# Strided attention feeding an FFN on one core: a new loop order for the strided copies to x^T, and one mask for a whole strided pair

## The chip, the cores and the metric

The kernel runs on one core of a Trainium2 chip. A core has TensorE (PE, matmuls), VectorE (DVE), ScalarE (ACT), GpSimd (POOL) and a queue engine (SP) that issues transfers; each engine works through its own list of instructions in order, and they wait for each other by semaphores. The metric is the device time of one execution, in microseconds (us).

## The reference

Eight batches of eight heads, 576 tokens, 64 values per head. Heads 0 to 3 see the last 32 tokens ("local"), heads 4 to 7 see the earlier tokens of the same class modulo 32 ("strided", at most 18 tokens a class). Then a gated FFN with no bias.

```python
scores = q @ k^T / sqrt(64)
rel = pos[:, None] - pos[None, :]
mask_local   = (rel >= 0) & (rel < 32)                  # heads 0..3
mask_strided = (rel >= 0) & (pos[None, :] % 32 == pos[:, None] % 32)   # heads 4..7
attn = softmax(where(mask, scores, -1e9));  o = attn @ v
x = o as [4608, 512]
out = (((x @ w1) * (x @ w2)) @ w3) @ w_out
```

## The kernel before, in words

w3 and w_out are folded into one matrix `w34` near the start, so each of the nine tiles of 512 tokens needs two products with w1 and w2 (L496, L507), their product on VectorE (L510) and one product with `w34` (L523). The FFN reads x^T, held as four tiles `xT`, one for each pair of heads.

Attention goes by pairs of heads: in each batch two local pairs (p0, p1) and two strided ones (p2, p3). Batches 0 and 1 use an older path (`ah_...`), at the start. From batch 2 on (`s.b >= AHEAD`) a strided pair puts its tokens in five chunks: four of 126 tokens (XW), of which chunk c (0 to 3) holds the tokens t*32 + a*4 + c with t = 0..17 and a = 0..6; and one chunk of 72 (SQ) with the tokens of a = 7. In each chunk a token sees only those of its own class.

The steps of a pair, each a function:

- `ph_S` (L308): the scores, transposed, into two PSUM tiles, `sps` for all chunks but the last, `pt` for the last chunk. The same `pt` also takes the transposes of the next pair's q and k (`ph_T`), which are then copied to `qT` and `kT` (L77 and L79 are the line of a helper `copy`, for ScalarE and VectorE). Where the next pair is the first of a batch, `ph_T` also brings the last 64 tokens of all its heads ("rest").
- `ph_soft`: exp on ScalarE (L328), in two instructions, for the first chunks and the last, to `pte`; then the masks on VectorE (L331) to `ptm`. A local pair needs one multiplication of 128x1152; a strided one has two, 126x1008 with `maskX` (126 columns, repeated eight times) and 72x144 with `maskS` (72 columns, twice).
- `ph_PV` (L344): `ptm` times v, with a column of ones beside v that gives the sums; `norm` divides on VectorE (L453 reciprocal, L454 to `xqs`).
- `ph_T2` (L462): transposes back, into one PSUM tile `ps`, and the copy to `xT`. For a local pair VectorE copies 576 contiguous values (L79). For a strided pair ScalarE copies twice: 504 values of the chunks of 126 (L470), and 72 values of the last chunk (L471). Within a row of `xT` token t*32 + a*4 + c is a value of two bytes at that place, while `ps` holds (c, t, a) in order.

PE's order is written out by hand. A list `stream` holds, for each pair, scores with the next pair's transposes, six gaps, PV, five gaps, T2, one gap. `host` spreads the FFN's parts of the tile before into these gaps. So an FFN tile and the attention of the batch that the next tile needs run interleaved, and in a batch PE comes to PV of p3 twelve L523 matmuls after its scores, and to T2 of p3 ten matmuls after PV. On the other engines a scheduler settles the order when the kernel is compiled.

The masks are made once. `maskS` comes at the start (L109). `maskX` is made just ahead of batch 2's own first pair, as the product of a small PE matmul (`xps`) with a causal triangle, on VectorE (L751).

Of the kernel before, what the change touches and what calls it, by code (L numbers as in the profile page):

```python
# [9 lines left out]
FP16 = mybir.dt.float16  # L10
AF = mybir.ActivationFunctionType
# [3 lines left out]
def _ap(t: bass.AP, off_add, dims):  # L15
    return bass.AP(tensor=t.tensor, offset=t.offset + off_add, ap=dims)
# [3 lines left out]
def kernel(  # L20
# [11 lines left out]
    nc = tc.nc  # L32
    B, H, S, D = q.shape
# [3 lines left out]
    P = 128  # L37
# [4 lines left out]
    scale = 1.0 / float(D) ** 0.5  # L42
# [5 lines left out]
    LQ, LT = 96, 6  # L48
    SQ, ST = 72, 8
# [4 lines left out]
    LC = 384  # L54
    XW, XN = 126, 4
    XC = XW * XN
# [3 lines left out]
    consts = ctx.enter_context(tc.tile_pool(name="consts", bufs=1))  # L60
# [11 lines left out]
    def pe(ins):  # L72
        return tc.keep_in_program_order(ins)

    def copy(eng, out, in_):
        if eng == "a":
            nc.scalar.copy(out=out, in_=in_)  # L77
        elif eng == "v":
            nc.vector.tensor_copy(out=out, in_=in_)  # L79
        else:  # L80
            nc.gpsimd.tensor_copy(out=out, in_=in_)  # L81
# [6 lines left out]
    maskL = consts.tile([P, LQ], FP16)  # L88
# [16 lines left out]
    maskS = consts.tile([SQ, SQ], FP16)  # L105
# [12 lines left out]
    v16S = [t[0:SQ].rearrange("p (h c e) -> p h c e", h=4, c=ST) for t in v16R]  # L118
    v16X = [t[:, 0:16 * (D + 1)].rearrange("p (h c e) -> p h c e", h=4, c=XN) for t in v16R]
    v16Y = [t[0:SQ, 16 * (D + 1):20 * (D + 1)].rearrange("p (h e) -> p h e", h=4) for t in v16R]  # L120
    maskX = consts.tile([XW, XW], FP16)


    qT = consts.tile([P, 4, S], FP16)
# [108 lines left out]
    for b in range(B):  # L233
        for hp in range(4):
            s = Pair()
# [62 lines left out]
    def ph_S(s):  # L298
        w, kr, n, n1 = s.w, s.kr, s.n, s.n1
        sps = psB.tile([P, 2, NB], FP32, tag="big", name="sps")  # L300
        pt = psB.tile([P, 2, NB], FP32, tag="big", name="pt")
        s.ps = sps

        def sc(h, c):
            r = half_rows(h)
            l = w if c < n1 else s.wl
            o = sps[:, h, c * w:c * w + l] if c < n1 else pt[:, h, LC:LC + l]
            pe(nc.tensor.matmul(o, kT[r, s.hp, w * c:w * c + P], qT[r, s.hp, w * c:w * c + l],  # L308
                                start=True, stop=True))

        for i in range(n):
            sc(0, (i - 1) % n)
            sc(1, i)

        def soft():
            ph_soft(s, pt)

        return pt, soft

    def ph_soft(s, pt):  # L320
        w, kr, n, n1 = s.w, s.kr, s.n, s.n1
        sps = s.ps
        pte = att.tile([P, 2 * S], FP16, tag="pte", bufs=2)
        ptm = s.ptm = ptms[s.hp % 2]
        m1 = 2 * n1 * w
        kl = kr if s.local else SQ
        for r, lo, hi, src in ((kr, 0, m1, sps[0:kr, 0:2, 0:n1 * w]), (kl, m1, 2 * S, pt[0:kl, :, LC:LC + s.wl])):
            nc.scalar.activation(out=pte[0:r, lo:hi], in_=src, func=AF.Exp, bias=0.0, scale=scale)  # L328
        for r, lo, hi, x, mk in (((P, 0, 2 * S, LQ, maskL),) if s.local else
                                 ((XW, 0, m1, XW, maskX), (SQ, m1, 2 * S, SQ, maskS))):  # L330
            nc.vector.tensor_mul(ptm[0:r, lo:hi].rearrange("p (a x) -> p a x", x=x),  # L331
                                 pte[0:r, lo:hi].rearrange("p (a x) -> p a x", x=x),
                                 _ap(mk, 0, [[mk.ap[0][0], r], [0, (hi - lo) // x], [1, x]]))

    def ph_PV(s):
        w, kr, n, n1 = s.w, s.kr, s.n, s.n1
        vt = (v16L if s.local else v16X)[s.b % 2]
        s.xqs = att.tile([P, ST, 2, D], FP16, tag="xqs", bufs=2, name="xqs")
        for c in range(n):
            for h in range(2):  # L340
                hv = 2 * (s.hp % 2) + h
                c0 = (h * n1 + c) * w if c < n1 else 2 * n1 * w + h * s.wl
                k, vv = (SQ, v16Y[s.b % 2][:, hv]) if not s.local and c == XN else (kr, vt[0:kr, hv, c, :])
                pe(nc.tensor.matmul(s.ps[:, h, c * 65:c * 65 + 65], s.ptm[0:k, c0:c0 + P], vv,  # L344
                                    start=True, stop=True))
        norm(s, s.ps[0:w, :, 0:n * 65], 0, n)
# [102 lines left out]
    def norm(s, xv, c0, l):  # L449
        w = s.w  # L450
        rcp = att.tile([P, 2, ST], FP32, tag="rcp")
        xv = xv.rearrange("p h (i e) -> p h i e", e=65)
        nc.vector.reciprocal(out=rcp[0:w, :, 0:l], in_=xv[:, :, :, D])  # L453
        nc.vector.tensor_mul(s.xqs[0:w, c0:c0 + l].rearrange("p i h d -> p h i d"), xv[:, :, :, 0:D],  # L454
                             _ap(rcp, 0, [[rcp.ap[0][0], w], [ST, 2], [1, l], [0, D]]))

    def ph_T2(s):
        w, n = s.w, s.n
        ps = psM.tile([P, 1024], FP16, tag="m")
        for t in range(n):  # L460
            l = w if t < n - 1 else s.wl
            pe(nc.tensor.transpose(ps[:, t * w:t * w + l],  # L462
                                   s.xqs[0:l, t].rearrange("p h d -> p (h d)"),
                                   id16[0:l, 0:l]))
        o = xT[s.hp][:, S * s.b:S * s.b + S]
        if s.local:
            copy("a" if s.b < AHEAD else "v", o, ps[:, 0:S])
        elif w == XW:
            ov = o.rearrange("x (t a c) -> x c t a", a=8, c=4)
            nc.scalar.copy(out=ov[:, :, :, 0:7], in_=ps[:, 0:XC].rearrange("x (c t a) -> x c t a", c=4, a=7))  # L470
            nc.scalar.copy(out=o.rearrange("x (t r) -> x t r", r=32)[:, :, 28:32],  # L471
                           in_=ps[:, XC:S].rearrange("x (t c) -> x t c", c=4))
        else:
            nc.scalar.copy(out=o.rearrange("x (p c) -> x p c", c=n),  # L474
                           in_=ps[:, 0:S].rearrange("x (c p) -> x p c", p=w))
# [4 lines left out]
    def ab_parts(tch):  # L480
        tok = bass.ds(tch * NT, NT)
        res = []

        def first():
            abts[tch] = ffn.tile([P, KF, NT], FP16, tag="abt", bufs=4, name=f"abt{tch}")

        for jc in range(KF):
            st = {}

            def a(qt, jc=jc, st=st):  # L490
                if qt == 0:
                    if jc == 0:
                        first()
                    st["a"] = psF.tile([P, NT], FP32, tag="f", name="aps")
                for ci in (2 * qt, 2 * qt + 1):
                    pe(nc.tensor.matmul(st["a"], w1h[:, ci, bass.ds(jc * P, P)], xT[ci][:, tok],  # L496
                                        start=(ci == 0), stop=(ci == KM - 1)))
                if qt:
                    asb = ffn.tile([P, NT], FP32, tag="asb")
                    nc.scalar.copy(out=asb, in_=st["a"])  # L500
                    st["asb"] = asb

            def bb(qt, jc=jc, st=st):
                if qt == 0:
                    st["b"] = psF.tile([P, NT], FP32, tag="f", name="bps")
                for ci in (2 * qt, 2 * qt + 1):
                    pe(nc.tensor.matmul(st["b"], w2h[:, ci, bass.ds(jc * P, P)], xT[ci][:, tok],  # L507
                                        start=(ci == 0), stop=(ci == KM - 1)))
                if qt:
                    nc.vector.tensor_mul(abts[tch][:, jc, :], st["b"], st["asb"])  # L510

            res += [lambda f=f, qt=qt: f(qt) for f in (a, bb) for qt in range(2)]
        return res
# [15 lines left out]
    def o_parts(tch):  # L529
        res = []  # L530
        for ts in range(NT // P):
            def done(ps, ts=ts):
                osb = ffn.tile([P, DM], FP32, tag="osb", bufs=3)
                nc.scalar.copy(out=osb, in_=ps)  # L534
                nc.scalar.dma_start(out_r[tch * (NT // P) + ts], osb)

            if tch + 1 < NTILE or ts + 1 < NT // P:
                res += acc_parts(lambda ci, ts=ts: abts[tch][:, ci, bass.ds(ts * P, P)],
                                 lambda ci: w34[:, ci, :], done, 4)
        return res  # L540
# [80 lines left out]
    add(ah_PV, p1, 0)  # L621
    add(ah_PV, p1, 1)
    add(ph_T2, p0)
    add(ah_T, p2)
    add(ph_T2, p1)
# [23 lines left out]
    for p, s in enumerate(pairs):  # L649
# [3 lines left out]
        t = pairs[p + 1] if p + 1 < len(pairs) else None  # L653
# [86 lines left out]
    causalX = selX[0:XW, P:P + XW]  # L740
# [7 lines left out]
                            pattern=[[1, XW]], channel_multiplier=-1)  # L748
    xps = psF.tile([P, 512], FP32, tag="f", name="mxps")
    pe(nc.tensor.matmul(xps[0:XW, 0:XW], selX[0:7, 0:XW], selX[0:7, 0:XW], start=True, stop=True))  # L750
    nc.vector.tensor_mul(maskX, xps[0:XW, 0:XW], causalX)  # L751
    tile1 = ab_parts(1) + o_parts(1)
    stream[pos[0]]()
    tile1[0]()
# [54 lines left out]
```

## Time and profile before

Three runs took 282.64, 283.52 and 285.09 us; the median is 283.52. The profiled execution took 282.21 us, of which the span from the first to the last instruction is 280.5.

| | us | note |
|---|---|---|
| profiled execution | 282.21 | span 280.5, TensorE clock granted in full |
| PE busy | 261.0 | 93% of the span |
| VectorE busy | 148.7 | 53% |
| ScalarE busy | 157.0 | 56% |
| GpSimd busy | 114.0 | 41%, none after 185 us |
| L470, copies of 504 to x^T | 17.4 | 12 of 1450 ns, all on ScalarE |
| L471, copies of 72 to x^T | 4.3 | 12 of 357 ns |
| L331, strided masks | 9.7 and 6.0 | 12 of 809 ns, 12 of 500 ns on average |
| L331, local masks | 11.0 | 12 of 915 ns on average |
| L328, exp | 12.2 and 3.4 | strided pairs: 12 of 1015 ns, 12 of 281 ns |

How to read it: a group's mean covers instructions that ran alone and ones that ran beside others. The shortest of the masks are 682 and 219 ns (strided) and 759 ns (local), the longest 1392, 1066 and 1421 ns. The profile names an instruction by its line, engine, operation and tiles; what an engine waited for is inferred from semaphores. Idle time of an engine that is not the bottleneck costs nothing by itself.

### The profile page before, as it was taken

Reading aid. Unit: us, or ns where it says so; the run is one execution under the profiler, and the core shown is the slowest. Engines: PE = TensorE matmul, PEld = TensorE weight load, DVE = VectorE, ACT = ScalarE, POOL = GpSimd, SP = SyncE. Lnnn points to the kernel's source line nnn. Section 1 sums busy time; section 2 is a strip of 40 time slices with the busy share of each in tenths; the row PEclk is TensorE's granted clock in tenths of the full one; section 3 lists DMA queues with packets and bytes.
Section 4 is the critical chain, followed back from the end, with each engine's and each line's share of the span. In section 5 each row is a group of like instructions: output and inputs, shape, how many; then the busy total and the mean of one; then the engine's idle time right before and its main releaser. Section 6 shows DMA issues by size and latency. Waiting matters only on the chain.

```text
span 280.5 us, 6375 instructions
## 1 busy us (share of the span) xinstructions
PE 261.0 (93%) x2477; PEld 135.2 (48%) x2477; DVE 148.7 (53%) x306; ACT 157.0 (56%) x322; POOL 114.0 (41%) x139
## 2 busy tenths in 40 slices
PE   1789999999899999998998999999999999999995
PEld 0465455555455445544554455445544544444442
DVE  2665342747677448745875477467447743320320
ACT  2663335766655765576656665766676664333322
POOL 4677775878817837648349258100000000000000
PEclk9999999999999999999999999999999999999999
DMA  7999999998749599299399396210031003004003
GB/s 208 271 336 390 394 385 241 246 218 211 267 161 252 147 313 280 71 275 307 54 271 278 131 271 193 112 41 2 1 115 40 0 25 127 0 0 153 0 0 150
DMA packets 60170, 48.65 MB, mean 173 GB/s; under 512 B 31324, under 2 KB 50988, under 8 KB 60140
## 3 DMA queue, kind: packets, MB, share of 16 engines
q1 hardware_dynamic: 54956, 38.87, 53.0%
q10 hardware_dynamic: 5184, 9.37, 8.9%
q8 instruction: 19, 0.31, 0.5%
q14 instruction: 11, 0.09, 0.1%
HBM read 38.80 MB, written 9.44 MB: 172 GB/s over the span
## 4 chain that ended last, share of the span: by engine, by line
PE 55%; DMA 13%; ACT 10%; DVE 9%; issue 8%; POOL 2%; SPq 1%; ACTq 1%; POOLq 0%; DVEq 0%
PE bps L507 18%; PE aps L496 17%; PE ops L523 10%; DMA st<-in_moe_w_out_dram 4%; DMA st<-in_k_dram 4%; ACT pte L328 3%; DMA st<-in_moe_w_dram 3%; DVE ptm L331 3%; PE ps L462 3%; PE sps L344 3%; DVE xqs L454 2%; DVE kT L79 2%; DMA st<-in_v_dram 2%; ACT osb L534 2%; ACT xT L471 2%
## 5 line engine op out<-in xcount | busy, mean ns | idle before, releaser
L507 PE MATMUL bps<-xT,w2h 128*128 128x512 f16 x288 | 76.2, 379 | 0.0
L496 PE MATMUL aps<-xT,w1h 128*128 128x512 f16 x288 | 75.1, 380 | 1.2 <-ACT xT L474 0.7
L510 DVE TENSOR_TENSOR abt<-bps,asb 128x512 f16<-128x512 f32 x72 | 49.4, 686 | 37.7 <-PE bps L507 28.0
L523 PE MATMUL ops<-w,abt 128*128 128x512 f16 x280 | 67.1, 379 | 0.0
L500 ACT COPY asb<-aps 128x512 f32<-128x512 f32 x72 | 42.3, 599 | 42.9 <-PE aps L496 33.6
L81 POOL CAST t<-st 128x1024 f16<-128x1024 f32 (+1 forms) x46 | 46.1, 1009 | 32.2 <-DMA st<-in_q_dram 17.0
L496 PEld LDWEIGHTS <-w1h 128*128 128x128 f16 x288 | 26.5, 98 | 29.7
L507 PEld LDWEIGHTS <-w2h 128*128 128x128 f16 x288 | 26.2, 98 | 28.3 <-issue 1.2
L523 PEld LDWEIGHTS <-abt 128*128 128x128 f16 x280 | 25.3, 98 | 26.3
L199 POOL CAST v16L<-st 32x768 f16<-32x768 f32 (+1 forms) x32 | 27.5, 860 | 8.4 <-DMA st<-in_v_dram 6.0
L328 ACT ACTIVATE pte<-sps 128x960 f16<-128x960 f32 (+1 forms) x24 | 23.9, 994 | 11.9 <-PE sps L308 11.9
L470 ACT COPY xT<-ps 128x504 f16<-128x504 f16 x12 | 17.4, 1450 | 18.8 <-PE ps L462 18.8
L534 ACT COPY osb<-ops 128x512 f32<-128x512 f32 x35 | 20.8, 594 | 12.7 <-PE ops L523 12.3
L331 DVE TENSOR_TENSOR ptm<-pte,maskL 128x1152 f16<-128x1152 f16 x12 | 11.0, 915 | 24.6 <-ACT pte L328 24.6
L331 DVE TENSOR_TENSOR ptm<-pte,maskX 126x1008 f16<-126x1008 f16 x12 | 9.7, 809 | 23.8 <-ACT pte L328 23.8
L454 DVE TENSOR_TENSOR xqs<-sps,rcp 96x768 f16<-96x768 f32 (+1 forms) x24 | 21.3, 889 | 0.8
L77 ACT COPY qT<-pt 128x224 f16<-128x224 f16 (+4 forms) x60 | 17.6, 352 | 4.8 <-DVE kT L79 4.4
L79 DVE COPY kT<-pt 128x512 f16<-128x512 f16 (+4 forms) x48 | 14.1, 325 | 4.5 <-ACT qT L77 3.1
L462 PEld LDWEIGHTS <-xqs 96*128 96x128 f16 (+2 forms) x188 | 11.3, 97 | 10.1 <-DVE xqs L454 4.0
L523 PE MATMUL ops<-woh,w3T 128*128 128x512 f16 x64 | 15.7, 380 | 0.2 <-DVE w3T L567 0.2
L344 PEld LDWEIGHTS <-ptm 128*128 128x128 f16 (+2 forms) x264 | 10.6, 97 | 10.8 <-DVE ptm L331 8.0
L462 PE MATMUL ps<-id,xqs 96*128 96x96 f16 (+2 forms) x188 | 13.5, 207 | 1.7 <-DVE xqs L454 1.6
(104 smaller groups left out, 262.8 us busy)
## 6 DMA issues: line engine op xcount, KB each, us to landing
out_dram<-osb ACTq DMA_DIRECT2D x35, 256.0 KB
st<-in_q_dram SPq DMA_DIRECT2D x16, 512.0 KB
st<-in_k_dram SPq DMA_DIRECT2D x16, 512.0 KB
st<-in_moe_w_dram SPq DMA_DIRECT2D x16, 512.0 KB
st<-in_v_dram SPq DMA_DIRECT2D x32, 144.0 KB
st<-in_v_dram SPq DMA_DIRECT2D x24, 112.0 KB
st<-in_moe_w_out_dram SPq DMA_DIRECT2D x4, 512.0 KB
st<-in_q_dram SPq DMA_DIRECT2D x8, 128.0 KB
```

Of the source, the lines that this page charges most:

```text
L81: nc.gpsimd.tensor_copy(out=out, in_=in_)
L199: nc.gpsimd.tensor_copy(out=vt[pr, hs, :, 0:D], in_=st[pr])
L328: nc.scalar.activation(out=pte[0:r, lo:hi], in_=src, func=AF.Exp, bias=0.0, scale=scale)
L331: nc.vector.tensor_mul(ptm[0:r, lo:hi].rearrange("p (a x) -> p a x", x=x), pte[0:r, lo:hi].rearrange("p (a x) -> p a x", x=x), _ap(mk, 0, ...
L454: nc.vector.tensor_mul(s.xqs[0:w, c0:c0 + l].rearrange("p i h d -> p h i d"), xv[:, :, :, 0:D], _ap(rcp, 0, [[rcp.ap[0][0], w], [ST, 2], [ ...
L462: pe(nc.tensor.transpose(ps[:, t * w:t * w + l], s.xqs[0:l, t].rearrange("p h d -> p (h d)"), id16[0:l, 0:l]))
L496: pe(nc.tensor.matmul(st["a"], w1h[:, ci, bass.ds(jc * P, P)], xT[ci][:, tok], start=(ci == 0), stop=(ci == KM - 1)))
L500: nc.scalar.copy(out=asb, in_=st["a"])
L507: pe(nc.tensor.matmul(st["b"], w2h[:, ci, bass.ds(jc * P, P)], xT[ci][:, tok], start=(ci == 0), stop=(ci == KM - 1)))
L510: nc.vector.tensor_mul(abts[tch][:, jc, :], st["b"], st["asb"])
L523: pe(nc.tensor.matmul(st["ps"], lhs(ci), rhs(ci), start=(ci == 0), stop=(ci == KF - 1)))
L534: nc.scalar.copy(out=osb, in_=ps)
```

## The change

Five places are edited, all of them for strided pairs from batch 2 on, but that the layout of `pte` and `ptm` is also changed for local ones.

- `ph_T2`: both copies to x^T run through (c, a, t), with the token class's 18 values of t innermost, where before the first ran through (c, t, a) and the second through (t, c). In `xT` the step of the innermost loop is now 32 values (64 bytes); before it was 4 values (8 bytes) in the first copy, and in the second the four values of c were adjacent. The number of values is as it was.
- `maskX` has 576 columns: four copies of the 126 columns, and `maskS` in the last 72, with zeros below it (partitions 72 to 125).
- `ph_soft`: `pte` and `ptm` hold head 0 in columns 0 to 575 and head 1 in 576 to 1151, all five chunks in a row, and one multiplication of 126x1152 takes the place of the two. The exp of the last chunk works on 126 partitions, before on 72.
- `ph_PV`: the column of a chunk follows the new layout; the matmuls are the same.
- Where `maskX` is made: a memset, four multiplications in place of one, and a copy of `maskS`.

```diff
-    maskX = consts.tile([XW, XW], FP16)
+    maskX = consts.tile([XW, S], FP16)
...
-        m1 = 2 * n1 * w
-        kl = kr if s.local else SQ
-        for r, lo, hi, src in ((kr, 0, m1, sps[0:kr, 0:2, 0:n1 * w]), (kl, m1, 2 * S, pt[0:kl, :, LC:LC + s.wl])):
-            nc.scalar.activation(out=pte[0:r, lo:hi], in_=src, func=AF.Exp, bias=0.0, scale=scale)
-        for r, lo, hi, x, mk in (((P, 0, 2 * S, LQ, maskL),) if s.local else
-                                 ((XW, 0, m1, XW, maskX), (SQ, m1, 2 * S, SQ, maskS))):
-            nc.vector.tensor_mul(ptm[0:r, lo:hi].rearrange("p (a x) -> p a x", x=x),
-                                 pte[0:r, lo:hi].rearrange("p (a x) -> p a x", x=x),
-                                 _ap(mk, 0, [[mk.ap[0][0], r], [0, (hi - lo) // x], [1, x]]))
+        pv = pte.rearrange("p (h x) -> p h x", h=2)
+        for lo, hi, src in ((0, n1 * w, sps[0:kr, 0:2, 0:n1 * w]), (n1 * w, S, pt[0:kr, :, LC:LC + s.wl])):
+            nc.scalar.activation(out=pv[0:kr, :, lo:hi], in_=src, func=AF.Exp, bias=0.0, scale=scale)
+        x, mk = (LQ, maskL) if s.local else (S, maskX)
+        nc.vector.tensor_mul(ptm[0:kr, 0:2 * S].rearrange("p (a x) -> p a x", x=x),
+                             pte[0:kr].rearrange("p (a x) -> p a x", x=x),
+                             _ap(mk, 0, [[mk.ap[0][0], kr], [0, 2 * S // x], [1, x]]))
...
-                c0 = (h * n1 + c) * w if c < n1 else 2 * n1 * w + h * s.wl
+                c0 = h * S + c * w
...
-            ov = o.rearrange("x (t a c) -> x c t a", a=8, c=4)
-            nc.scalar.copy(out=ov[:, :, :, 0:7], in_=ps[:, 0:XC].rearrange("x (c t a) -> x c t a", c=4, a=7))
-            nc.scalar.copy(out=o.rearrange("x (t r) -> x t r", r=32)[:, :, 28:32],
-                           in_=ps[:, XC:S].rearrange("x (t c) -> x t c", c=4))
+            ov = o.rearrange("x (t a c) -> x c a t", a=8, c=4)
+            nc.scalar.copy(out=ov[:, :, 0:7], in_=ps[:, 0:XC].rearrange("x (c t a) -> x c a t", c=4, a=7))
+            nc.scalar.copy(out=ov[:, :, 7], in_=ps[:, XC:S].rearrange("x (t c) -> x c t", c=4))
...
-    nc.vector.tensor_mul(maskX, xps[0:XW, 0:XW], causalX)
+    nc.vector.memset(maskX[:, XC:S], 0.0)
+    for c in range(XN):
+        nc.vector.tensor_mul(maskX[:, c * XW:(c + 1) * XW], xps[0:XW, 0:XW], causalX)
+    nc.vector.tensor_copy(out=maskX[0:SQ, XC:S], in_=maskS)
```

## The prediction

> **What bounds the kernel now.** I read the page's engine table first, then the waits of PE, then the timeline around the strided pairs. PE is busy for 261.0 of 280.5 us, at full granted clock, so only the time in which PE stands still can be won.
>
> ```profile
> PE 261.0 (93%) x2477; PEld 135.2 (48%) x2477; DVE 148.7 (53%) x306; ACT 157.0 (56%) x322; POOL 114.0 (41%) x139
> ```
>
> By the windows view 11.7 us of PE's idle time lie before 76 us, where input transfers and start-up chains rule, and 3.3 us behind 277, the last output; this change touches neither much. From 76 to 237 us the timeline (start, length, engine, line, operation; in brackets the idle time before it and what ended that) shows PE's idle stretches, which I add up by cause. All but one are of three kinds:
>
> ```profile
> 96.36 0.27 PE L344 MATMUL sps<-v16S,ptm 126*128 126x65 f16 x3 [0.60 <-DVE ptm L331]
> ...
> 99.11 0.43 PE L462 MATMUL ps<-id,xqs 126*128 126x126 f16 x5 [0.33 <-DVE xqs L454]
> ...
> 130.94 0.54 PE L344 MATMUL sps<-v16L,ptm 128*128 128x65 f16 x12 [0.86 <-DVE ptm L331]
> ```
>
> First kind: PV of the second strided pair (p3) waits for its mask: 0.60, 0.39 and 0.15 = 1.14 us in all. Second: T2 of p3 waits for the normalised rows `xqs`: 0.33, 0.24, 0.33, 0.22, 0.24 = 1.36 us. Third: PV of the next batch's first local pair waits for its mask, 0.20, 0.86, 0.18, 0.18, 0.18 = 1.60 us. Once, at the end, the FFN waits 0.50 us for the last copy to x^T (L471). Together 4.6 us: that is all that this stage can give. The first and third kinds hang on ScalarE: `pte` (exp) stands in its queue behind the two copies to x^T of the pair before:
>
> ```profile
> 119.41 1.45 ACT L470 COPY xT<-ps 128x504 f16<-128x504 f16 x1 [1.56 <-PE ps L462]
> 120.56 0.36 ACT L471 COPY xT<-ps 128x72 f16<-128x72 f16 x1
> 120.74 0.60 ACT L534 COPY osb<-ops 128x512 f32<-128x512 f32 x1
> 121.23 1.02 ACT L328 ACTIVATE pte<-sps 126x1008 f16<-126x1008 f32 x1
> ```
>
> The scores for that exp were ready at about 120.2; it starts at 121.23. So ScalarE's two copies are on the path, and what they cost decides.
>
> **Part 1: the copies to x^T.** ScalarE copies that write contiguously lie on a line: 56 elements 218 ns, 512 elements 595, 576 elements (L474) 642, so 172 ns + 0.827 ns per element. Some of them read PSUM with 128-byte (L77) or 144-byte (L474) steps and still lie on it, so the new stepped read of PSUM is costed at nothing. L470 writes single fp16 values 8 bytes apart; by the line its 504 elements are 588 ns, it takes 1450: 862 ns too many, or 2.54 ns per element. L471, with groups of four adjacent values 64 bytes apart, ends 57 ns after L470 (120.92 against 120.86): its 72 elements go at 0.8 ns each, 3.2 ns for each group. From the start of L470 to the next instruction 1.33 us pass.
>
> After the change all 576 values are written singly, 64 bytes apart. No ScalarE row shows that, so bounds:
>
> - Low end: the line for both. The nearest row for single fp16 writes at a wide step is VectorE's memset of every 65th value (130 bytes), L130 and L132 below (shortest, median and longest ns): 24 values 78 ns, 32 values 85 ns, so under 1 ns for each further one. Then the two copies take 576 x 0.827 + 2 x 0.10 (between two `asb` copies in a row, 1.12 us for both, 0.525 us pass from start to start, 0.10 more than 512 x 0.827) = 0.68 us: x = -0.65 us per strided pair.
>
> ```profile
> L470 ACT COPY xT<-ps x12: 1436/1449/1460, 91.7 to 234.7; 128x504 f16<-128x504 f16 x12
> ...
> L130 DVE MEMSET v16L<- x2: 78/78/78, 1.1 to 1.3; 128x24 f16 x2
> ...
> L132 DVE MEMSET v16S<- x2: 85/85/85, 1.2 to 2.0; 126x32 f16 x2
> ```
>
> - Middle: 2.54 ns for each single value wherever it goes. L470 stays, L471 pays 72 x (2.54 - 0.8): x = +0.12.
> - High end: each new place costs what a group of L471 costs, 3.2 ns. 504 x (3.2 - 2.54) + 72 x (3.2 - 0.8) = 0.33 + 0.17: x = +0.50.
>
> I take the low end: of the two rows with wide steps both go fast (0.8 and under 1 ns per value), and only the row with the 8-byte step is slow, which looks like a cost of neighbouring writes that don't join.
>
> The Trainium skill (SBUF — State Buffer, Specifications) speaks against this change: lines of 16 bytes, two hits in a line needed for full speed, and each change of line paid. By it the old step of 8 bytes would be free and the new one not; the trace disagrees on the first half (1450 ns, not 588). Charging L470's 862 ns to its 288 line changes (3.0 ns each), the new copies would pay 504 and 72 of them: x = +0.86, and the sum below would be about +8.7 us.
>
> **Part 2: the mask.** Before: 684 + 224 ns, from 122.29 to 123.11 where GpSimd is idle. After: one operation of 126x1152, for which the local mask (128x1152, 765 ns) is the row: it ends 0.055 us before the second and 0.085 after the first, on which PV's first eight matmuls wait. So about +0.06 us where PV comes directly behind it (four of six batches, if the copies stay as slow as they are). Where GpSimd works beside it the old pair takes 0.92 + 0.85 (149.78 to 151.47), and the local mask 1.42 at worst; the merged one should end some 0.3 us earlier, twice. The exp of 126 instead of 72 partitions costs the same (281 ns). The new rows of `pte` cost nothing.
>
> **Part 3: the order on VectorE.** In the compiled instruction lists the four `kT` rest copies (0.54 us, behind a wait of 0.63 for `qT`) stand ahead of reciprocal and `xqs` of p3 before, and behind them after, in the five batches that have a next one:
>
> ```profile
> 124.34 0.54 DVE L79 COPY kT<-pt 128x128 f16<-128x128 f16 x4 [0.63 <-ACT qT L77]
> 124.80 0.21 DVE L453 RECIPROCAL rcp<-sps 126x10 f32<-126x10 f32 x1
> 125.04 0.82 DVE L454 TENSOR_TENSOR xqs<-sps,rcp 126x640 f16<-126x640 f32 x1
> ```
>
> `xqs` then starts at about 123.95 instead of 125.04 and ends at 124.8; PE reaches T2 at 125.68, when its ten matmuls are done. The second kind of stall goes: -1.36 us. What is moved back, `kT`, ends near 125.3; the scores that need it come at 126.7 (now with a wait of their own): 1.4 us of cover. On ScalarE an output's issue (0.34 us on the queue) moves ahead of the `qT` rest copies; the same cover hides it.
>
> **Part 4: making the mask.** Three more multiplications of 289 ns (L751's row) stand in VectorE's queue behind the `xqs` that ends at 71.92; they end by 72.8, the next mask comes at 73.63, and the PE matmul that now waits for their PSUM buffer comes at 73.70. Hidden by that idle time (1.71 us); without it, 0.9 us. The memset and the copy of `maskS`, some 0.1 us each (memset row 85 ns, `biasS` row 170 ns), fall to idle VectorE at 2.3 us and ahead of `kT` at 8.27; the next `kT` copy has 0.26 us of idle time before it. Nothing to +0.1.
>
> **Sum.** With x = -0.65 exp starts that much earlier, so the third kind (1.60) goes but for perhaps 0.1 beside GpSimd, the first (1.14) too, but for 0.2, and the last 0.50: 1.5 + 0.94 + 0.5 + 1.36 = 4.3, less 0.1 to 0.2 in the start: -4.1 us. What is late next is nothing before PE itself. Even half of that x gives about -3.4, since most stalls are short: the gain is capped. The profiled run took 282.21 us (span 280.5), 1.3 us below the median 283.52 of the three shown (282.64 to 285.09): 282.21 - 4.1 = 278.1, and **279.4 us** on the scale of the median.
>
> **The rivals.**
>
> - *A single write costs the same at any step* (x = +0.12). For: 2.54 ns is a plain price per value. Against: the memset row. Stalls of the second kind go (-1.36), the first gains 0.6 from the merged mask twice and loses 0.06 four times, and 0.12 is paid at 12 places (six PVs of p3, five of the next local pair, the end): -1.36 - 0.36 + 1.44 + 0.1 = -0.2: 283.3 us.
> - *Each new place is charged* (x = +0.50). For: the step is eight times wider, so nothing can join, and the bound from L471 allows it. Against: groups at the same 64-byte step ran without a surcharge. The exp has no slack (it already waits behind the copies), so 12 x 0.50 - 1.36 - 0.36 + 0.1 = +4.4: 287.9 us, slower. It turns slower than before from x = +0.14 on, by over 1% from x = +0.37. The Trainium skill's line rule (SBUF — State Buffer, Specifications) stands beside this rival, with the +8.7 given above: about 292.
> - *The copies get faster, but the time goes elsewhere*: the stalls are short (0.18 to 0.86 us) and PE's queue may hide or show them otherwise; with half the gain, 281.4 us.
>
> **Chances.** Forecast 0.50; same price 0.16; half the gain 0.10; each place charged 0.24, a third of it above the price from L471. The range runs from 277.6 (all 4.6 us gone from the profiled run's own 282.21) to 288.0 (the place-charged rival at its price), which leaves out what is charged above that price, and a little below. A change of 1%, about 2.8 us, is what a measurement of this kernel can tell from none. Faster by over 1%: the forecast and a bit of the half gain, 0.52; within 1%: 0.25; slower: 0.23.
>
> **What would show it.** The two copies' rows on ScalarE: 590 and 230 ns if right, 1450 and 350 or more if the price is per value, 1770 and 400 or more if each place is charged. T2's wait for `xqs` gone in every batch whatever the copies do. The merged mask at 765 ns, once per strided pair. PV's waits for `ptm` gone, or grown to about x more each. The forecast is wrong if ScalarE's wide single writes are slower than VectorE's.

## The result, and the profile after

The changed kernel took 293.59 us (median of four runs, 292.66 to 297.70), beside 283.81 us (median of four, 282.64 to 285.09) for the kernel before: ratio 1.033, with a 95% interval of 1.026 to 1.040. A run more than 1.5% above the fastest of its kernel, here the one of 297.70 us, is left out of this ratio and of those below. The changed kernel is slower by about 10 us; 279.4 had been forecast. The profiled execution took 294.32 us, of which the span is 292.6.

The copies to x^T did not get faster, they got slower. This is ScalarE's timeline in the changed kernel, in the same batch as the lines shown of before (start, length, engine, line, operation, in brackets the idle time before it and what ended that):

```profile
121.68 2.39 ACT L468 COPY xT<-ps 128x504 f16<-128x504 f16 x1 [2.14 <-PE ps L460]
...
123.56 0.82 ACT L469 COPY xT<-ps 128x72 f16<-128x72 f16 x1
...
123.88 0.93 ACT L531 COPY osb<-ops 128x512 f32<-128x512 f32 x1
...
124.69 1.02 ACT L327 ACTIVATE pte<-sps 126x1008 f16<-126x1008 f32 x1
```

The first copy takes 2.37 us (median) where it took 1.45, the second 0.81 where it took 0.36. From the start of the first copy to exp 3.01 us pass, before 1.82: x, the prediction's change per strided pair, is +1.19 us and not -0.65. From the start of the first copy to the end of the second it is 1.51 us before and 2.70 after, the same +1.19. To the start of the next instruction, as the prediction counted, only 0.87 more pass (1.33 and 2.20), but that instruction, the output's copy to `osb`, now takes 0.93 us where it took 0.60. PE's timeline shows who pays:

```profile
126.88 0.48 PE L342 MATMUL sps<-v16S,ptm 126*128 126x65 f16 x10 [1.39 <-ACT osb L531]
132.54 0.38 PE L493 MATMUL aps<-xT,w1h 128*128 128x512 f16 x1 [0.98 <-ACT xT L469]
134.85 0.54 PE L342 MATMUL sps<-v16L,ptm 128*128 128x65 f16 x12 [0.21 <-DVE ptm L329]
```

PV of the second strided pair (p3) stands still for 1.2 to 1.6 us in each batch, in the other batches with the mask as its releaser. The second line is a wait that came only once before, at the very end:

```profile
236.27 0.38 PE L496 MATMUL aps<-xT,w1h 128*128 128x512 f16 x1 [0.50 <-ACT xT L471]
```

The next FFN tile's first product with w1 is summed from four matmuls, and the last of them needs the part of x^T that this copy writes. It now waits about 1 us in every batch, and 1.66 at the end. T2's wait for `xqs` is gone everywhere.

I add PE's idle time by cause from each timeline, from the last matmul of tile 1's first FFN product on. This matmul has the same 0.15 us wait on x^T in every kernel (L496 at 74.67 before, L493 at 75.67 after), so that the stretch from there to the end of the span can be compared without the start-up, which differs by up to 3 us between the profiled executions (73.04 to 76.15 us). The last five rows are experiments, told below.

| kernel | PV of p3 | T2 of p3 | PV of next local pair | first FFN product | sum | stretch |
|---|---|---|---|---|---|---|
| before | 1.14 | 1.36 | 1.60 | 0.50 | 4.60 | 205.8 |
| after | 7.95 | 0 | 1.04 | 6.56 | 15.55 | 216.9 |
| `copies_alone` | 9.27 | 1.50 | 1.04 | 6.58 | 18.39 | 221.1 |
| `mask_alone` | 0.65 | 0 | 2.50 | 0.51 | 3.66 | 204.6 |
| `cin_alone` | 0 | 0 | 0 | 0 | 0 | 199.1 |
| `cin_mask` | 0 | 0 | 0 | 0 | 0 | 198.7 |
| `pairs_mask` | 0 | 0 | 0 | 0 | 0 | 198.9 |

The stretch grew by 11.1 us and the waits by 10.95: the loss is these waits. The other 1.0 us of the two profiled spans' difference of 12.1 lies ahead of the stretch. There the changed kernel's profiled run had a granted clock of 0.84 between 9 and 20 us, before 1.00. Two other runs of the changed kernel had a mean clock of 0.999 and 1.000 and took 292.86 or less, so that this seems to belong to the execution and not to the change.

### The profile page after: what moved, and what is told of

It reads as the page before. It is cut to its first block, busy times and chain, and to the rows that moved or that the text cites. A ratio compares the mean times of both kernels' runs of the same rounds, so it can differ in the third digit from the quotient of the medians.

```text
span 292.6 us, 6372 instructions
## 1 busy us (share of the span) xinstructions
PE 263.2 (90%) x2477; PEld 136.6 (47%) x2477; DVE 144.8 (49%) x299; ACT 171.9 (59%) x322; POOL 114.7 (39%) x139
## 4 chain that ended last, share of the span: by engine, by line
PE 60%; ACT 10%; DMA 9%; issue 8%; DVE 5%; SPq 4%; POOL 3%; ACTq 0%; POOLq 0%; DVEq 0%
PE bps L504 17%; PE aps L493 16%; PE ops L520 15%; DMA st<-in_v_dram 3%; ACT xT L469 3%; PE sps L342 3%; ACT pte L327 3%; PE ps L460 2%; DMA st<-in_q_dram 2%; DVE ptm L329 2%; ACT osb L531 2%; DMA out_dram<-osb 2%; SPq L197 1%; DMA sy<-in_v_dram 1%; PE tps L356 1%
## 5 line engine op out<-in xcount | busy, mean ns | idle before, releaser
L493 PE MATMUL aps<-xT,w1h 128*128 128x512 f16 x288 | 75.9, 380 | 7.2 <-ACT xT L469 6.6
L493 PEld LDWEIGHTS <-w1h 128*128 128x128 f16 x288 | 26.4, 98 | 29.7
L468 ACT COPY xT<-ps 128x504 f16<-128x504 f16 x12 | 28.4, 2368 | 17.9 <-PE ps L460 17.9
L531 ACT COPY osb<-ops 128x512 f32<-128x512 f32 x35 | 24.8, 708 | 13.6 <-PE ops L520 13.6
L327 ACT ACTIVATE pte<-sps 128x960 f16<-128x960 f32 (+1 forms) x24 | 23.9, 994 | 12.1 <-PE sps L308 12.1
L329 DVE TENSOR_TENSOR ptm<-pte,maskX 126x1152 f16<-126x1152 f16 x12 | 10.4, 865 | 34.2 <-ACT pte L327 34.2
L329 DVE TENSOR_TENSOR ptm<-pte,maskL 128x1152 f16<-128x1152 f16 x12 | 9.8, 819 | 31.7 <-ACT pte L327 31.7
L460 PEld LDWEIGHTS <-xqs 96*128 96x128 f16 (+2 forms) x188 | 11.9, 99 | 7.1 <-issue 0.2
```

Of the source, the lines that this page charges most:

```text
L327: nc.scalar.activation(out=pv[0:kr, :, lo:hi], in_=src, func=AF.Exp, bias=0.0, scale=scale)
L329: nc.vector.tensor_mul(ptm[0:kr, 0:2 * S].rearrange("p (a x) -> p a x", x=x), pte[0:kr].rearrange("p (a x) -> p a x", x=x), _ap(mk, 0, [[m ...
L460: pe(nc.tensor.transpose(ps[:, t * w:t * w + l], s.xqs[0:l, t].rearrange("p h d -> p (h d)"), id16[0:l, 0:l]))
L468: nc.scalar.copy(out=ov[:, :, 0:7], in_=ps[:, 0:XC].rearrange("x (c t a) -> x c a t", c=4, a=7))
```

## The experiments

**The change taken apart.** My theory after the result (A): all of the loss sits in the loop order of the two copies, and the rest of the change is a small gain. The rival (B): the new layout, the merged mask or the moved `kT` copies carry a part of it. One kernel has all but the copies, the other only the copies.

```diff
 # mask_alone: the changed kernel with
-            ov = o.rearrange("x (t a c) -> x c a t", a=8, c=4)
-            nc.scalar.copy(out=ov[:, :, 0:7], in_=ps[:, 0:XC].rearrange("x (c t a) -> x c a t", c=4, a=7))
+            ov = o.rearrange("x (t a c) -> x c t a", a=8, c=4)
+            nc.scalar.copy(out=ov[:, :, :, 0:7], in_=ps[:, 0:XC].rearrange("x (c t a) -> x c t a", c=4, a=7))
...
 # copies_alone: the kernel before with the opposite edit
```

> The changed kernel with the old loop order in both copies to x^T: the mask, the layout and VectorE's order are changed, the copies are not. Theory A (the whole loss sits in ScalarE's copies): the copies take 1450 and 357 ns as before, T2's waits for xqs (1.36 us) are gone, the waits of the second strided pair's PV shrink by about 0.3 us; some 1.6 us under the kernel before, 282.2 us, ratio 0.994. Rival B (the new layout, the merged mask or the kT copies moved behind xqs cost a part of the 9.8 us): above 285 us, with new waits of PE for kT, ptm or the first FFN matmuls.

> The kernel before with only the new loop order in the two copies to x^T. Theory A: the copies take 2370 and 810 ns, exp comes 1.2 us later after each strided pair, the changed kernel's waits appear and T2's 1.36 us stay: about 1.6 us above the changed kernel, 295 us, ratio 1.04. Rival B: the copies carry only a part, 286 to 291 us.

`mask_alone` took 280.42 us, ratio 0.990 (0.985 to 0.995); `copies_alone` 297.69 us, ratio 1.051 (1.048 to 1.055), more than the 295 us expected. Both kernels ran beside the same runs of before, 283.31 us. A holds and B falls: the copies alone lose more than the whole change, and the rest gains a little. The groups of `copies_alone` show the two copies at the same length as in the changed kernel:

```profile
L470 ACT COPY xT<-ps 128x504 f16<-128x504 f16 x12 | 28.4, 2367 | 20.3 <-PE ps L462 20.3
...
L471 ACT COPY xT<-ps 128x72 f16<-128x72 f16 x12 | 9.7, 806 | 0.0
```

The columns are busy us in all, mean ns of one, and the idle us before them. In the stretch, `mask_alone` gains 1.3 us, of which the table shows 0.9: T2's 1.36 and half of PV's 1.14 go, but the next local pair's PV waits 0.9 us longer. Its mask ran beside a GpSimd copy in two batches and took 1.47 and 1.62 us there, 0.76 where GpSimd was idle (waits of 0.90 and 1.05, in the others 0.18 or 0.19). I had expected 1.6. The measured times differ by 2.9 us, with an interval of 1.5 to 4.3; of the profiled spans' difference of 1.9, 0.6 lies ahead of the stretch. Whether the change does something there stays open.

**What the copies could cost.** If the write's pattern is what is paid for and the read is free, an order that writes as many adjacent values as possible must be fast: c innermost gives 28 adjacent values (a and c) at each t, read from PSUM with steps of 252 bytes.

```diff
-            ov = o.rearrange("x (t a c) -> x c a t", a=8, c=4)
-            nc.scalar.copy(out=ov[:, :, 0:7], in_=ps[:, 0:XC].rearrange("x (c t a) -> x c a t", c=4, a=7))
-            nc.scalar.copy(out=ov[:, :, 7], in_=ps[:, XC:S].rearrange("x (t c) -> x c t", c=4))
+            ov = o.rearrange("x (t a c) -> x t a c", a=8, c=4)
+            nc.scalar.copy(out=ov[:, :, 0:7], in_=ps[:, 0:XC].rearrange("x (c t a) -> x t a c", c=4, a=7))
+            nc.scalar.copy(out=ov[:, :, 7], in_=ps[:, XC:S].rearrange("x (t c) -> x t c", c=4))
```

> The kernel before with another loop order in the first copy to x^T: token class outermost, then a, and c innermost, so that 28 adjacent values are written in a row, 18 times, while PSUM is read with steps of 252 bytes; the second copy stays as it was. Theory A (a ScalarE write pays about 4.4 ns for each new place, reads at any step are free): the first copy falls from 1450 to about 590 ns, exp comes 0.65 us earlier, the waits of the next local pair's PV (1.6 us) and most of those of the second strided pair's PV and of the last copy go; T2's 1.36 us stay: 281.0 us, ratio 0.990. Rival C (the price is one of stepped access in general, reads included): the copy stays above 1400 ns, 283 to 288 us.

> The changed kernel with c innermost in the first copy to x^T (28 adjacent values in a row, 18 times) and the second copy as in the kernel before: both gains together. Theory A: copies of 590 and 230 ns, T2's waits gone too: 4.2 us under the kernel before, 279.6 us, ratio 0.985. Rival D (the stalls turn up elsewhere on PE once ScalarE is early): as cin_alone or above, ratio 0.99 to 1.00.

`cin_alone`, the old kernel with this edit, took 276.85 us: ratio 0.978 (0.973 to 0.983). `cin_mask`, the changed kernel with it, 274.12 us: ratio 0.969 (0.966 to 0.972). It beats both kernels of the case. ScalarE's groups in `cin_mask`:

```profile
L468 ACT COPY xT<-ps 128x504 f16<-128x504 f16 x12 | 6.9, 579 | 18.6 <-PE ps L460 18.6
...
L469 ACT COPY xT<-ps 128x72 f16<-128x72 f16 x12 | 2.7, 224 | 0.0
```

That is the line of the prediction (588 and 231 ns). C falls: reads at the steps tried are free here. D falls too: no wait turned up in another place. Two expectations missed. T2's waits went in `cin_alone` too, though VectorE's order there is the old one: with exp some 0.7 us earlier, `xqs` is earlier by as much (it starts 1.24 us after PV's start and not 1.98, in the batch of the lines shown), and T2 waited only 0.22 to 0.33. And the gain is larger than the 4.6 us of idle time that I had taken for the most that could be won: the stretch is 6.7 us shorter in `cin_alone`, 7.1 in `cin_mask`. PE's own row tells where the rest was (the engine table of `cin_mask`'s page; before had 261.0 us for the same matmuls):

```profile
PE 258.4 (95%) x2477; PEld 136.2 (50%) x2477; DVE 143.8 (53%) x299; ACT 150.2 (55%) x322; POOL 115.0 (42%) x139
```

The 2477 matmuls are busy for 2.6 us less. A matmul of 512 columns shows 0.38 us when it stands alone (L496 at 236.27, above), but twelve in a row take 2.76 us:

```profile
120.45 2.76 PE L523 MATMUL ops<-w,abt 128*128 128x512 f16 x12
```

That is (2.76 - 0.38) / 11 = 0.216 us each. So a wait shorter than about 0.16 us shows as no idle time at all, and a longer one shows that much too short. Before has 14 waits in the table's columns; 14 x 0.16 = 2.2 us, and 4.6 + 2.2 = 6.8 is close to what was won. The other kernels bear this out: in the stretch the same matmuls are busy for 195.4 to 195.8 us in the three kernels without a wait in the table, 197.3 in `mask_alone` (8 waits), 197.9 before (14), 198.1 after (17) and 199.5 in `copies_alone` (25), which is 0.15 to 0.22 us more for each wait. Once the copies are fast, the mask's part of the change is worth about 0.5 us in the stretch (199.1 to 198.7), by one profile of each.

**The price itself.** A kernel without attention and FFN timed copies of 504 fp16 values one by one, with many patterns of write.

```python
def step(k): return big[:, 0:N * k].rearrange("p (n k) -> p n k", k=k)[:, :, 0]
def grp(g, k): return big[:, 0:N // g * k].rearrange("p (n k) -> p n k", k=k)[:, :, 0:g]
for _ in range(4):
    nc.scalar.copy(out=step(32), in_=flat)        # and so on; flat is 504 values in PSUM
    nc.vector.tensor_copy(out=tiny[:, 0:1], in_=big[:, 0:1])
```

> No attention and no FFN: the output is filled with zeros, and beside it copies of 504 fp16 values from PSUM to SBUF are timed one by one (a small read by another engine lies between them), four of each kind. Theory A, ScalarE pays 172 ns + the larger of 0.827 ns per value and 4.4 ns per new place, a place being the 16-byte line of the Trainium skill's page SBUF - State Buffer (Specifications): adjacent 590; steps of 4 bytes 730, 8 bytes 1280, 16, 32, 64 and 130 bytes 2390 each; pairs every 8 bytes 730, every 16 bytes 1280; fours every 16 or 64 bytes 730; sevens and twelves every 64 bytes 590; the old order of the copy to x^T 1450, the new one 2370, c innermost 590; the new order's read with an adjacent write 590. Rival E (a price for each single write, growing with the distance, as banks that collide at 64 bytes would give): 16 and 130 bytes well under 64 bytes, below 1500. Rival F (the price is in the PSUM read): the new order's read with an adjacent write near 2370. VectorE: if the memset rows (under 1 ns per value at 130 bytes) hold for a long copy, 600 to 700 ns at every step; if it pays as ScalarE does, above 2300 at 64 and 130 bytes. GpSimd, from SBUF, is only looked at.

| ScalarE, 504 values | ns | expected |
|---|---|---|
| adjacent | 579 | 590 |
| single, every 4 bytes | 717 | 730 |
| single, every 8 bytes | 1272 | 1280 |
| single, every 16, 32, 64, 130 bytes | 2385, 2260, 2342, 2390 | 2390 |
| pairs, every 8 and every 16 bytes | 579, 601 | 730, 1280 |
| fours, every 16 and every 64 bytes | 579, 579 | 730 |
| sevens, twelves, every 64 bytes | 582, 579 | 590 |
| old order, new order, c innermost | 1430, 2344, 579 | 1450, 2370, 590 |
| new order's read, adjacent write | 580 | 590 |

E falls (no step from 16 bytes on is cheaper than another by more than 6%), and F falls (the read is free). Theory A is right for single values and wrong for pairs and fours: a new place as such is not what costs. Rows of the trace (L91 ScalarE, L133 VectorE and L145 GpSimd are single values every 64 bytes, L100 is ScalarE's pairs every 16 bytes):

```profile
L145 POOL COPY big<-ssb 128x504 f16<-128x504 f16 x4 | 9.5, 2371 | 1.0 <-DVE tiny L54 1.0
...
L91 ACT COPY big<-src 128x504 f16<-128x504 f16 x4 | 9.4, 2342 | 0.9 <-DVE tiny L54 0.9
L133 DVE COPY big<-src 128x504 f16<-128x504 f16 x4 | 9.4, 2342 | 1.0 <-ACT tiny L57 1.0
...
L100 ACT COPY big<-src 128x504 f16<-128x504 f16 x4 | 2.4, 601 | 0.9 <-DVE tiny L54 0.9
```

All three engines pay the same, so it isn't ScalarE's price. And VectorE's copy pays at 130 bytes as well (2390 ns), against the row that I had built on. GpSimd's lengths are the roughest of the profile, and its copies read SBUF and not PSUM.

**What is charged.** New theory (W): a two-byte value that leaves half of its 4-byte word unwritten is charged, once for each 16-byte place and each time that the walk comes to it, however many such values it then writes there: by the singles above 4 x 1.08, 2 x 2.18 and 1 x 4.39 ns for places with four, two and one of them ((717 - 172) / 504 and so on), 4.33 to 4.39 each time. The old order of the copy to x^T comes to a new place 288 times, 288 x 4.35 + 172 = 1425 ns (measured 1430); the new order comes to one with each of its 504 values, though their neighbours are written later (2344 ns). Whole words are not charged. The rival (P): two values at a place are enough, wherever the word's boundary lies. For the kernel, W says that the walk over 18 tokens at 64 bytes would be harmless if it wrote pairs; the rival there (G) is that the walk costs.

```diff
 # pairs_mask: the changed kernel with two adjacent c at each step of t
-            ov = o.rearrange("x (t a c) -> x c a t", a=8, c=4)
-            nc.scalar.copy(out=ov[:, :, 0:7], in_=ps[:, 0:XC].rearrange("x (c t a) -> x c a t", c=4, a=7))
+            ov = o.rearrange("x (t a c k) -> x c a t k", a=8, c=2, k=2)
+            pv = ps[:, 0:XC].rearrange("x (c k t a) -> x c a t k", c=2, k=2, a=7)
+            for c in range(2):
+                nc.scalar.copy(out=ov[:, c, 0:7], in_=pv[:, c])
...
 # steps2: as steps, with fp32 values, pairs from an odd value on, short copies, memsets
```

> The changed kernel, its 18 tokens still in the inner walk at 64-byte steps, but two adjacent values of c written at each step, so that whole 4-byte words are written; the first copy is split in two of 252 values each. Theory W (only values that leave a 4-byte word half written are charged, some 4.35 ns for each place of 16 bytes that they touch): the copies take about 380 ns twice and 230 ns, the time is that of cin_mask, 274.5 us, ratio 0.97. Rival G (the walk over the tokens at 64-byte steps is what costs): the copies take over 1100 ns each, 285 us or more.

> No attention and no FFN: the output is filled with zeros, and copies and memsets are timed one by one as in the run steps. Theory W, on ScalarE: fp32 values adjacent, every 16 bytes and every 64 bytes all near 580 ns; fp16 pairs that straddle two 4-byte words, every 16 and every 64 bytes, 172 + 252 x 4.35 = 1270 ns; pairs in one word every 64 bytes 600; the 504 adjacent values shifted by one value 580; threes every 64 bytes 172 + 168 x 4.35 = 900; 24, 72 and 144 single values at 130 bytes 276, 485 and 800. Rival P (the word's boundary doesn't matter, two values at a place are enough): straddling pairs near 600. VectorE's memsets at 130-byte steps, the rows that I had built on: if memset pays too once it is long, 128 values about 600 ns and 504 values about 2300; if it is never charged, about 180 and 570. VectorE's copy of 32 single values at 130 bytes against 32 adjacent ones: 110 to 140 ns more if short copies pay in full, under 20 more if the first few dozen are absorbed.

`pairs_mask` took 275.28 us, ratio 0.973 (0.967 to 0.978), with copies of 376 (twice) and 239 ns and no wait left: the walk is harmless, G falls.

```profile
L470 ACT COPY xT<-ps 128x252 f16<-128x252 f16 x24 | 7.8, 376 | 18.1 <-PE ps L460 18.1
...
L471 ACT COPY xT<-ps 128x72 f16<-128x72 f16 x12 | 2.9, 239 | 0.0
```

The rows of `steps2`:

```profile
L100 ACT COPY big<-src 128x504 f16<-128x504 f16 x4 | 5.1, 1281 | 0.1
...
L94 ACT CAST big<-src 128x504 f32<-128x504 f16 x4 | 4.2, 1042 | 0.9 <-DVE tiny L79 0.9
...
L106 ACT COPY big<-src 128x504 f16<-128x504 f16 x4 | 2.3, 580 | 0.7 <-DVE tiny L56 0.7
...
L133 DVE MEMSET big<- 128x504 f16 x4 | 1.9, 478 | 8.4 <-issue 8.4
...
L136 DVE COPY big<-src 128x32 f16<-128x32 f16 x4 | 1.2, 300 | 1.0 <-ACT tiny L59 1.0
...
L139 DVE COPY big<-src 128x32 f16<-128x32 f16 x4 | 0.7, 174 | 1.0 <-ACT tiny L59 1.0
```

L100 are pairs every 16 bytes that straddle two words: 1281 ns (median 1272, expected 1270), where the pairs within a word took 601, and at 64 bytes 1252 against 580 (L106). Only the start was shifted by one value. P falls. The two halves of such a pair lie in one place and are charged once, (1281 - 172) / 252 = 4.40 ns. Threes every 64 bytes took 888 ns (expected 900), 24, 72 and 144 single values 266, 477 and 797 (276, 485, 800). L94, fp32 values every 16 bytes, missed: 1042 ns and not 580, (1042 - 172) / 504 = 1.73 ns for each, and 999 at 64 bytes. So one whole word at a place does cost something, about two values' time, but not the 4.35. With fp16 pairs this can't be seen, since the two values take that time anyway ((601 - 172) / 252 = 1.70 ns a pair).

L133 is VectorE's memset of 504 single values at 130 bytes: 478 ns, no charge at all. L136 and L139 are VectorE's copies of 32 values, single at 130 bytes and adjacent: 126 ns more, 3.9 for each value. A copy pays from the first values on; a memset doesn't.

## Why the prediction was wrong

- **The bound was read rightly**: PE, the stretch behind 76 us, and ScalarE's two copies. But the loss came by two paths: 6.8 us by way of exp and the mask to PV of p3, as the prediction had it, and 6.1 us by the FFN product that reads x^T itself, which it had only at the end.
- **The step that failed is the low end of part 1**, taken as x = -0.65 us. Measured were +1.19: the copies took 2.37 and 0.81 us and not 0.59 and 0.23. The memset of every 65th value was the nearest row by its step, but it was another operation, and memsets are not charged (478 ns for 504 values) where copies on the same engine are (2390 ns). The other row with a wide step, L471, was fast for a reason that I had not seen: its groups of four fill whole words. "Only the row with the 8-byte step is slow" had the right fact; what set it apart was single values, not near neighbours.
- **The bounds of x were too narrow as well.** The 3.2 ns of the high end were worked out from whole words. By the price measured, 504 x 4.36 - 1278 ns = 0.92 us, and 72 x (4.36 - 0.83) = 0.25: x = +1.17, which the trace has as 1.19. The rival "each new place is charged" (0.24) was nearest; what happened is its part above the price from L471, to which the prediction gave a third of that.
- **The rule that stood against the change was nearer than the row that I chose.** The Trainium skill (SBUF — State Buffer, Specifications) says that a 16-byte line needs at least two hits for full bandwidth and that each change of line is paid. Priced from L470 it gave x = +0.86 and about 292 us; 293.59 was measured, but the price of 3.0 ns was low as well. The 16-byte place is confirmed (4.33 to 4.39 ns a place with four, two or one single value), and so are two hits where whole words are written (pairs 601 ns, fp32 singles 1042). It doesn't hold for single fp16 values every 8 bytes: two hits, 1272 ns. I took this failure on the old step as grounds to doubt the rule on the new one, and no row supported that.
- **The working from x to the time came out near, in part by luck.** With 1.19 in "12 x - 1.36 - 0.36 + 0.1" it gives +12.7 us; the stretch grew by 11.1. But five of the twelve places were other than I said: the first FFN product waits in each batch, not only at the end, and the PV of the next local pair, which comes behind it, waits less than before (1.04 us against 1.60).
- **The mask (part 2)** ran at 759 ns against 765 expected, **the order on VectorE (part 3)** took T2's 1.36 us away as worked out, with no wait for `kT`, and **making the mask (part 4)** delayed nothing: from the small matmul that it needs to the FFN matmul with the 0.15 us wait 4.01 us pass before (70.66 to 74.67) and after (71.66 to 75.67). Together they gained 1.3 us in the stretch of `mask_alone`, where the sum said 1.7; the longer local masks beside GpSimd were not in it.
- **The cap of 4.6 us was too low.** Waits under 0.16 us don't show, and each longer one shows 0.16 too little; 7.1 us were to be had.

## What to carry to other kernels

When fp16 is scattered in SBUF by a copy, order the loops so that the innermost writes fill aligned 4-byte words, pairs at the least, and let the strided side be the read from PSUM; walking a dimension at a wide step costs nothing by itself where at least a pair is written at each step (580 ns for pairs every 64 bytes), while single fp32 values still pay a little (999). To price a write pattern that the trace lacks, take a row of the same kind of instruction, and where the rows with the nearest pattern differ in kind, keep the slow one as the bound. Idle time between matmuls understates a wait by the difference between a lone matmul's length and its share in a row.

## What the runs showed of the hardware

- A copy's two-byte value that leaves half a 4-byte word unwritten costs about 4.35 ns for each 16-byte place, each time that the walk comes to it, on ScalarE, VectorE and GpSimd alike (2342, 2342 and 2371 ns for 504 values every 64 bytes; adjacent 579, 421 and 608).
- Whether a pair fills one word or straddles two decides: 601 against 1272 ns.
- VectorE's memset does not pay: 504 single values at 130 bytes in 478 ns, 128 in 165, so 0.83 ns for each further one. Why it differs from a copy was not tried.
- A step in the PSUM read costs ScalarE nothing: 580 ns with the new order's read, 579 with steps of 252 bytes.
